# Moving the K and V loads of an attention decode kernel from SyncE's queue to GpSimd, marked as one packet

## The chip, the cores and the metric

The kernel runs on one core of a Trainium2 chip. A core has five engines with instruction streams of their own: TensorE (PE, matmuls and weight loads), VectorE (DVE), ScalarE (ACT), GpSimd (POOL) and SyncE (SP). They meet through semaphores. Data come from HBM, the chip's main memory, into SBUF, the on-chip memory of 128 partitions, by DMA: an engine's instruction stream issues a transfer, and the core's 16 DMA engines carry it out in packets. The metric is the device time of one execution in microseconds (us).

## The reference

One token is decoded. An attention block with 32 heads reads a cache of 65,536 keys and values of 128 elements for each head, a small gated feed-forward block (SwiGLU) reads the same token, and a scalar gate mixes the two.

```python
def _A_ref(x, k_cache, v_cache, wq, wo):
    B, Sq, D = x.shape                      # 1, 1, 512
    H, Dh = 32, 128
    q = (lambda x, *d: x.transpose(*d))((x @ wq).reshape(B, Sq, H, Dh), 0, 2, 1, 3)
    scores = jnp.einsum("bhqd,bhkd->bhqk", q, k_cache) * (Dh ** -0.5)
    p = _softmax(scores, axis=-1)
    o = jnp.einsum("bhqk,bhkd->bhqd", p, v_cache)
    return (lambda x, *d: x.transpose(*d))(o, 0, 2, 1, 3).reshape(B, Sq, H * Dh) @ wo
...
g = _sigmoid((x * gate_w).sum(-1, keepdims=True))
a = _A_ref(x, A_k_cache, A_v_cache, A_wq, A_wo)
b = _B_ref(x, B_w_gate, B_w_up, B_w_down)
return g * a + (1 - g) * b
```

All tensors are bf16. K and V together are about 1.07 GB, and every byte is read once.

## The kernel before, in words

A head's K is 128 partitions by 512 rows of 128 elements. It is cut into two halves, called z = 0 and z = 1, of 256 rows for each partition: 64 KB for each partition, 8.39 MB in all. V is cut the same way. One load brings one half, so a head takes four loads. They all land in one large SBUF tensor, `mem`, which is addressed in units of 1 KB (lines 49, 84 and 109): K's half 0 lies at 32 to 95, its half 1 at 0 to 63 (head 0's half 1 at 96 to 159), V's half 0 at 120 to 183 and its half 1 at 96 to 159. The places overlap, so a load may start only when parts of the half that lies there have been consumed.

**The work of a head.** VectorE transposes a half of K in eight pieces (lines 322, 415 and 422) into the two buffers of `kt`; each transpose adds one to the semaphore `ktdone`. TensorE multiplies each piece with the query (line 472) and adds one to `qkdone`, which allows the transpose after the next. After sixteen pieces the maximum is taken, ScalarE computes the exponentials (line 288), and VectorE spreads them for the value matmuls (line 331). The value matmuls (line 525) come in four parts for each head, and each part adds one to `pvdone`. They run one head behind the scores: in TensorE's loop, head i's scores stand between the parts of head i - 1's values.

**The order of the loads.** SyncE's instruction stream (lines 220 to 263) issues nearly every transfer, so they all go into one queue, q1. The order is written out by hand: first the weights wq, w_gate, w_up, w_down (line 213), then K of head 0 half 0 in two pieces (line 228), then half 1 after the query is ready (`s_q`), then a fixed order in which each load stands behind a wait for the work that frees its place. For head 1's K half 0 that is `ktdone` of 8; for head 0's V half 0, `ktdone` of 13 and `s_b`; for head 1's K half 1, `ktdone` of 20; for head 0's V half 1, `pvdone` of 5. The loop of line 241 repeats the four loads for the next thirty heads (K two heads and V one head ahead of the loop's counter), with waits on constants that grow with the counter. Each load adds 16 to its semaphore when it has landed: `ka`, `kz`, `va`, `vz` for K and V, half 0 and 1.

**The end.** After the loop SyncE waits for `ktdone` of 504 and loads wo (line 251), then the last head's V in eight pieces of falling size (`tail`, line 61, issued on line 258), then two small parts of wo (lines 260 and 261) and the output. GpSimd's stream holds nothing of the kernel's own.

Of the kernel before, what the change touches and what calls it, by code (L numbers as in the profile page):

```python
# [21 lines left out]
def bass_gated_mix__mha_block_cached__swiglu_ffn__decode_kernel(  # L22
# [11 lines left out]
    out: bass.AP,  # L34
):
    _, H, S, Dh = A_k_cache.shape
    D = A_wq.shape[0]
    F = B_w_gate.shape[1]
# [3 lines left out]
    HR = R // 2  # L42
    NP = HR // PR
# [21 lines left out]
    with ExitStack() as ctx:  # L65
# [6 lines left out]
        def sem(name):  # L72
            return ctx.enter_context(nc.semaphore(name))
# [35 lines left out]
        def at(kb, n):  # L109
            return mem[:, kb * KB:kb * KB + n]  # L110
# [7 lines left out]
        mrow, amx, Lt = psM[0:1, 0:128], psM[:, 256:257], psM[:, 257:258]  # L118
        gm = sc[0:1, 5:6]

        names = ("x", "gw", "wq", "wg", "wu", "wd", "ka0", "ka", "kz", "va", "vz", "wo", "wj", "w31")
        d = {n: sem("d_" + n) for n in names}
        dt_ = [sem(f"d_t{i}") for i in range(len(tail))]
        s_ones = sem("s_ones")
# [23 lines left out]
        s_b = sem("s_b")  # L148
        s_dch = sem("s_dch")
        ktdone = sem("ktdone")  # L150
        qkdone = sem("qkdone")
        pvdone = sem("pvdone")
# [48 lines left out]
        def place(kind, h, z):  # L201
            if kind == "k":
                return (KA, V0)[z] if isinstance(h, int) and h == 0 else (KA, KZ)[z]
            return (VA, VZ)[z]

        def kv_dram(cache, h):
            if isinstance(h, int):
                return cache[0, h].rearrange("(b p r) d -> b p (r d)", b=2, p=P)
            return cache[0, ds(h, 1)].rearrange("a (b p r) d -> b (a p) (r d)", b=2, p=P)
# [8 lines left out]
        block = ctx.enter_context(nc.Block())  # L218

        @block.sync  # L220
        def _(sp):
            def load(kind, h, z):
                cache = A_k_cache if kind == "k" else A_v_cache
                sp.dma_start(at(place(kind, h, z), HR * Dh), kv_dram(cache, h)[z]).then_inc(d[kind + "az"[z]], 16)  # L224

            half = HR // 2 * Dh
            for n in range(2):
                sp.dma_start(at(KA + 32 * n, half), kv_dram(A_k_cache, 0)[0][:, n * half:n * half + half]).then_inc(
                    (d["ka0"], d["ka"])[n], 16)
            sp.wait_ge(s_q, 1)  # L230
            load("k", 0, 1)
            sp.wait_ge(ktdone, NP)
            load("k", 1, 0)
            sp.wait_ge(ktdone, 2 * NP - 3)
            sp.wait_ge(s_b, 1)
            load("v", 0, 0)
            sp.wait_ge(ktdone, 2 * NP + NP // 2)
            load("k", 1, 1)
            sp.wait_ge(pvdone, 5)
            load("v", 0, 1)  # L240
            with nc.sync.Fori(0, H - 2) as i:
                sp.wait_ge(ktdone, i * (2 * NP) + (4 * NP - 4))
                load("k", i + 2, 0)
                sp.wait_ge(pvdone, i * 4 + 7)
                load("v", i + 1, 0)
                sp.wait_ge(ktdone, i * (2 * NP) + (4 * NP + NP // 2))
                load("k", i + 2, 1)
                sp.wait_ge(pvdone, i * 4 + 9)
                load("v", i + 1, 1)
            sp.wait_ge(ktdone, 2 * NP * H - NP)  # L250
            sp.dma_start(at(WO, 31 * D), w_dram["wo"][:, 0:31 * D]).then_inc(d["wo"], 16)
            src = A_v_cache[0, H - 1].rearrange("(b p r) d -> b p (r d)", b=2, p=P)
            need = {0: (ktdone, 2 * NP * H - 4), 1: (ktdone, 2 * NP * H), 2: (pvdone, 4 * H - 1)}
            for n, (kb, r0, nr) in enumerate(tail):
                if n in need:
                    sp.wait_ge(*need[n])
                b, o = divmod(r0, HR)
                sp.dma_start(at(kb, nr * Dh), src[b][:, o * Dh:(o + nr) * Dh]).then_inc(dt_[n], 16)
            sp.wait_ge(pvdone, 4 * H)
            sp.dma_start(at(WOJ, D), wj_dram).then_inc(d["wj"], 16)  # L260
            sp.dma_start(at(WO31, D), w31_dram).then_inc(d["w31"], 16)
            sp.wait_ge(s_fin, 1)
            sp.dma_start(out_dram[2:4, :], fin[32:34, :]).then_inc(s_out2, 16)

        @block.scalar
        def _(act):
# [38 lines left out]
        def _(dve):  # L305
# [5 lines left out]
                dve.wait_ge(s_dch, chain[0])  # L311

            def transposes(z):
                dve.wait_ge(d[("ka0", "kz")[z]], 16)
                for c, u in enumerate(k_order[z]):
                    i = NP * z + c
                    if i == NP // 2:
                        dve.wait_ge(d["ka"], 16)
                    if i >= 2:
                        dve.wait_ge(qkdone, i - 1)  # L320
                    src = at(place("k", 0, z) + 8 * u, PR * Dh).bitcast(U32)
                    nc.vector.transpose(kt[:, i % 2, :].rearrange("p (j r t) -> p r j t", j=2, t=32),  # L322
                                        src.rearrange("p (r j t) -> p r j t", j=2, t=32)).then_inc(ktdone, 1)

            def shuffle(z, s):
                c0 = 256 * z
                for g in range(4):
                    for b in range(4):
                        dst = pb[32 * g:32 * g + 32, c0:c0 + 256].rearrange("p (n b) -> p n b", b=4)[:, :, b]
                        sr = pa[32 * b:32 * b + 32, c0:c0 + 256].rearrange("p (n g) -> p n g", g=4)[:, :, g]  # L330
                        last = nc.vector.tensor_copy(dst, sr)  # L331
                last.then_inc(s, 1)

            def top(h, qk):
                dve.wait_ge(qkdone, qk)
                nc.vector.reduce_max(mxs, psS[:], AX_X).then_inc(s_mx, 1)  # L336
                dve.wait_ge(s_mt, h + 1)
                nc.vector.reduce_max(gm, mrow, AX_X).then_inc(s_gm, 1)  # L338

            def late(pv, sl, so):  # L340
                dve.wait_ge(pvdone, pv)
                shuffle(1, s_pbz)
                dve.wait_ge(s_L, sl)
                dve.wait_ge(s_or, so)
                nc.vector.reciprocal(Li, Lt).then_inc(s_li, 1)
# [52 lines left out]
            link(nc.vector.tensor_tensor(hbuf[:, 1, 0:FC], hbuf[:, 0, 0:FC], psM[:, 80:80 + FC], ALU.mult))  # L398
            nc.vector.tensor_scalar(guT[:, 0:FC], hbuf[:, 1, 0:FC], gcol[:, 1:2], None, ALU.mult).then_inc(s_gu, 1)
            transposes(0)  # L400
            transposes(1)
            top(0, 2 * NP)
            with nc.vector.Fori(1, H) as i:
                n = i * (2 * NP)
                v = i * 4
                dma = i * 16
                dve.wait_ge(d["ka"], dma + 16)
                for c, u in enumerate(k_order[0]):
                    if c == NP // 2:
                        dve.wait_ge(expdone, i)  # L410
                        dve.wait_ge(pvdone, v - 2)
                        shuffle(0, s_pba)
                    dve.wait_ge(qkdone, n + (c - 1))
                    src = at(KA + 8 * u, PR * Dh).bitcast(U32)
                    nc.vector.transpose(kt[:, c % 2, :].rearrange("p (j r t) -> p r j t", j=2, t=32),  # L415
                                        src.rearrange("p (r j t) -> p r j t", j=2, t=32)).then_inc(ktdone, 1)
                late(v, i, i)
                dve.wait_ge(d["kz"], dma + 16)
                for c, u in enumerate(k_order[1]):
                    dve.wait_ge(qkdone, n + (NP + c - 1))  # L420
                    src = at(KZ + 8 * u, PR * Dh).bitcast(U32)
                    nc.vector.transpose(kt[:, c % 2, :].rearrange("p (j r t) -> p r j t", j=2, t=32),  # L422
                                        src.rearrange("p (r j t) -> p r j t", j=2, t=32)).then_inc(ktdone, 1)
                top(i, n + 2 * NP)
# [206 lines left out]
```

## Time and profile before

| what | value |
|---|---|
| runs (3), device time | 2513.89 to 2513.92 us, median 2513.9 us |
| profiled execution, span from the first to the last instruction | 2512.4 us |
| median of the runs less the span | 1.5 us |
| granted TensorE clock, mean | 0.721 of full speed |
| HBM read in the profiled execution | 1087.77 MB |

How to read it: the span is one profiled execution; the runs are timed on their own. The page lists busy times of the engines, a strip of 40 equal slices of the span, the DMA queues with their packets, the chain of work that ended last, and the groups of instructions that cost most. The suffix q, as in SPq, marks an engine's instruction stream where it issues a transfer. In a timeline a row is: start, duration, engine, line, operation, output<-input, count, and in brackets the idle time before it with what ended it; repeated instructions are merged, so a row of x2 spans from the first start to the last end.

### The profile page before, as it was taken

Reading aid. Unit: us, or ns where it says so; the run is one execution under the profiler, and the core shown is the slowest. Engines: PE = TensorE matmul, PEld = TensorE weight load, DVE = VectorE, ACT = ScalarE, POOL = GpSimd, SP = SyncE. Lnnn points to the kernel's source line nnn. Section 1 sums busy time; section 2 is a strip of 40 time slices with the busy share of each in tenths; the row PEclk is TensorE's granted clock in tenths of the full one; section 3 lists DMA queues with packets and bytes.
Section 4 is the critical chain, followed back from the end, with each engine's and each line's share of the span. In section 5 each row is a group of like instructions: output and inputs, shape, how many; then the busy total and the mean of one; then the engine's idle time right before and its main releaser. Section 6 shows DMA issues by size and latency. Waiting matters only on the chain.

```text
span 2512.4 us, 51694 instructions
## 1 busy us (share of the span) xinstructions
PE 1709.8 (68%) x21624; PEld 978.8 (39%) x21624; DVE 1411.8 (56%) x1683; ACT 64.6 (3%) x195; POOL 0.2 (0%) x4
## 2 busy tenths in 40 slices
PE   4666766667667677676676766766767767677677
PEld 3334433333433344333443333343334333344334
DVE  4764565554655645646456555465564564645653
ACT  0000000000000000000000000000000000000000
POOL 0000000000000000000000000000000000000000
PEclk8667767777677677776776767767767677677677
DMA  9999999999999999999999999999999999999999
GB/s 420 436 434 434 434 435 434 434 434 434 434 434 434 434 434 434 434 434 434 434 434 434 434 434 434 434 434 434 434 434 434 434 434 434 435 434 434 434 435 402
DMA packets 20470, 1087.93 MB, mean 433 GB/s; under 512 B 2282, under 2 KB 2668, under 8 KB 2924
## 3 DMA queue, kind: packets, MB, share of 16 engines
q1 hardware_dynamic: 20452, 1087.78, 100.0%
q8 instruction: 9, 0.15, 0.0%
q14 instruction: 1, 0.01, 0.0%
q10 hardware_dynamic: 8, 0.00, 0.0%
HBM read 1087.77 MB, written 0.00 MB: 433 GB/s over the span
## 4 chain that ended last, share of the span: by engine, by line
DMA 70%; PE 27%; DVE 1%; issue 1%; SPq 0%; ACT 0%; DVEq 0%
DMA mem<-in_A_v_cache_dram 67%; PE psO L525 27%; DMA mem<-in_A_k_cache_dram 2%; DMA mem<-in_A_wo_dram 1%; DVE kt L322 1%; DMA mem<-in_A_wq_dram 0%; DVE kt L415 0%; SPq L224 0%; PE psM L456 0%; DVE pb L331 0%; PE psS L472 0%; PE psM L547 0%; DVE sm L336 0%; PE psZ L600 0%; PE psM L549 0%
## 5 line engine op out<-in xcount | busy, mean ns | idle before, releaser
L472 PE MATMUL psS<-qcur,kt 128*128 128x4 bf16 x16384 | 573.0, 169 | 728.3 <-DVE kt L415 414.2
L525 PE MATMUL psO<-mem,pb 128*4 128x512 bf16 x3968 | 1040.6, 428 | 32.9 <-DMA mem<-in_A_v_cache_dram 32.6
L472 PEld LDWEIGHTS psS<-qcur,kt 128*128 128x128 bf16 x16384 | 534.0, 105 | 791.9 <-issue 789.5
L422 DVE STREAM_TRANSPOSE kt<-mem 128x2048 uint32<-128x2048 uint32 x248 | 547.6, 2275 | 402.3 <-DMA mem<-in_A_k_cache_dram 402.3
L415 DVE STREAM_TRANSPOSE kt<-mem 128x2048 uint32<-128x2048 uint32 x248 | 551.3, 2280 | 240.3 <-DMA mem<-in_A_k_cache_dram 239.3
L525 PEld LDWEIGHTS psO<-mem,pb 128*4 128x4 bf16 x3968 | 359.4, 93 | 657.5 <-issue 238.4
L331 DVE COPY pb<-pa 32x64 bf16<-32x64 bf16 x1024 | 233.5, 228 | 15.1 <-ACT pa L288 1.5
L338 DVE TENSOR_REDUCE sc<-psM 1x1 f32<-1x128 f32 x32 | 8.9, 279 | 334.9 <-PE psM L547 334.9
L336 DVE TENSOR_REDUCE sm<-psS 128x1 f32<-128x512 f32 x32 | 22.1, 692 | 42.3 <-PE psS L472 42.3
L322 DVE STREAM_TRANSPOSE kt<-mem 128x2048 uint32<-128x2048 uint32 x16 | 35.4, 2277 | 17.0 <-DMA mem<-in_A_k_cache_dram 17.0
L286 ACT ACTIVATE sm<-psM 128x1 f32<-128x1 f32 x32 | 5.5, 171 | 1222.7 <-PE psM L549 1222.7
L282 ACT ACTIVATE oTn<-psT,gcol 128x1 f32 (+1 forms) x31 | 8.2, 264 | 1035.1 <-PE psT L499 1035.1
L499 PE MATMUL psT<-ident,orow 4*128 4x1 f32 x256 | 33.5, 248 | 0.5 <-ACT orow L280 0.5
L499 PEld LDWEIGHTS psT<-ident,orow 4*128 4x128 f32 x256 | 30.8, 186 | 1.2 <-ACT orow L280 0.6
L280 ACT ACTIVATE orow<-psO,sm 4x512 f32<-4x512 f32 x31 | 21.0, 677 | 130.3 <-PE psO L525 126.0
L288 ACT ACTIVATE pa<-psS,sm 128x512 bf16<-128x512 f32 x32 | 22.0, 687 | 1.0
L549 PE MATMUL psM<-sc,onesf 1*128 1x1 f32 x64 | 12.3, 259 | 11.9 <-DVE sc L338 11.9
L561 PE MATMUL psW<-pb,mem 128*128 128x1 bf16 x512 | 14.5, 164 | 5.2 <-DMA mem<-in_A_v_cache_dram 4.7
L549 PEld LDWEIGHTS psM<-sc,onesf 1*128 1x128 f32 x64 | 9.6, 186 | 21.5 <-DVE sc L338 21.5
L561 PEld LDWEIGHTS psW<-pb,mem 128*128 128x128 bf16 x512 | 13.9, 100 | 6.4 <-issue 4.2
L553 PEld LDWEIGHTS psM<-sm,onesf 128*128 128x128 f32 x64 | 9.7, 191 | 14.7 <-issue 13.5
L553 PE MATMUL psM<-sm,onesf 128*128 128x1 f32 x64 | 12.5, 264 | 1.1 <-ACT pa L288 1.1
(72 smaller groups left out, 94.0 us busy)
## 6 DMA issues: line engine op xcount, KB each, us to landing
mem<-in_A_v_cache_dram SPq DMA_DIRECT2D x3, 4096.0 KB, 29.4
mem<-in_A_k_cache_dram SPq DMA_DIRECT2D x2, 4096.0 KB, 38.7
mem<-in_A_wq_dram SPq DMA_DIRECT2D x1, 4096.0 KB, 12.3
mem<-in_A_wo_dram SPq DMA_DIRECT2D x1, 3968.0 KB, 36.7
mem<-in_A_v_cache_dram SPq DMA_DIRECT2D x1, 2048.0 KB, 31.2
mem<-in_B_w_gate_dram SPq DMA_DIRECT2D x1, 1792.0 KB, 16.0
mem<-in_B_w_up_dram SPq DMA_DIRECT2D x1, 1792.0 KB, 21.0
mem<-in_B_w_down_dram SPq DMA_DIRECT2D x1, 1792.0 KB, 24.7
```

The lines of the kernel that those rows point to most:

```text
L288: nc.scalar.activation(pa[:], psS[:], ACT.Exp, bias=nbias, scale=SCALE, accum_out=rsum).then_inc(expdone, 1)
L322: nc.vector.transpose(kt[:, i % 2, :].rearrange("p (j r t) -> p r j t", j=2, t=32), src.rearrange("p (r j t) -> p r j t", j=2, t=32)).then ...
L331: last = nc.vector.tensor_copy(dst, sr)
L336: nc.vector.reduce_max(mxs, psS[:], AX_X).then_inc(s_mx, 1)
L415: nc.vector.transpose(kt[:, c % 2, :].rearrange("p (j r t) -> p r j t", j=2, t=32), src.rearrange("p (r j t) -> p r j t", j=2, t=32)).then ...
L422: nc.vector.transpose(kt[:, c % 2, :].rearrange("p (j r t) -> p r j t", j=2, t=32), src.rearrange("p (r j t) -> p r j t", j=2, t=32)).then ...
L472: last = nc.tensor.matmul(psS[:, o:o + 4] if j is None else psS[:, ds(j * (2 * PR) + o, 4)], ktb[b][:, je // 2, r, :, je % 2], qcur[:, je, ...
L499: last = nc.tensor.matmul(psT[:, 0:1], orow[0:4, i * Dh:(i + 1) * Dh], ident[0:4, i:i + 1], start=(i == 0), stop=(i == 3))
L525: last = nc.tensor.matmul(psO[0:4, :], pb[:, k_col[256 * z + r]:k_col[256 * z + r] + 4], vt[:, r * Dh:(r + 4) * Dh], start=(z == 0 and par ...
L549: nc.tensor.matmul(amx, onesf[0:1, :], gm, start=True, stop=True).then_inc(s_ar, 1)
L553: nc.tensor.matmul(Lt, onesf[:], rsum, start=True, stop=True).then_inc(s_L, 1)
L561: last = nc.tensor.matmul(psW[:, 0:1], vt[:, r * Dh:(r + 1) * Dh], pb[:, col:col + 1], start=(r0 + r == 0), stop=(r0 + r == R - 1))
```

## The change

The loads of K from head 1 on and of V up to head 30, 62 each, leave SyncE's stream and go, with the same waits in the same order, into a stream of GpSimd, with `single_packet=True`. SyncE keeps the weights, all of head 0's K, wo and the pieces of the last head's V. Head 0's K gets semaphores of its own (`ka0`, `ka1`, `kz0`), so that `ka` and `kz` count GpSimd's loads alone, and VectorE's waits for them count from 16 for head 1.

```diff
-        names = ("x", "gw", "wq", "wg", "wu", "wd", "ka0", "ka", "kz", "va", "vz", "wo", "wj", "w31")
+        names = ("x", "gw", "wq", "wg", "wu", "wd", "ka0", "ka1", "kz0", "ka", "kz", "va", "vz", "wo", "wj", "w31")
...
         @block.sync
         def _(sp):
-            def load(kind, h, z):
-                cache = A_k_cache if kind == "k" else A_v_cache
-                sp.dma_start(at(place(kind, h, z), HR * Dh), kv_dram(cache, h)[z]).then_inc(d[kind + "az"[z]], 16)
-
             half = HR // 2 * Dh
             for n in range(2):
                 sp.dma_start(at(KA + 32 * n, half), kv_dram(A_k_cache, 0)[0][:, n * half:n * half + half]).then_inc(
-                    (d["ka0"], d["ka"])[n], 16)
+                    (d["ka0"], d["ka1"])[n], 16)
             sp.wait_ge(s_q, 1)
-            load("k", 0, 1)
-            sp.wait_ge(ktdone, NP)
-            load("k", 1, 0)
...
-            with nc.sync.Fori(0, H - 2) as i:
...
+            sp.dma_start(at(place("k", 0, 1), HR * Dh), kv_dram(A_k_cache, 0)[1]).then_inc(d["kz0"], 16)
             sp.wait_ge(ktdone, 2 * NP * H - NP)
             sp.dma_start(at(WO, 31 * D), w_dram["wo"][:, 0:31 * D]).then_inc(d["wo"], 16)
...
+        @block.gpsimd
+        def _(gp):
+            def gload(kind, h, z):
+                cache = A_k_cache if kind == "k" else A_v_cache
+                gp.dma_start(at(place(kind, h, z), HR * Dh), kv_dram(cache, h)[z],
+                             single_packet=True).then_inc(d[kind + "az"[z]], 16)
+
+            gp.wait_ge(ktdone, NP)
+            gload("k", 1, 0)
+            gp.wait_ge(ktdone, 2 * NP - 3)
+            gp.wait_ge(s_b, 1)
+            gload("v", 0, 0)
+            gp.wait_ge(ktdone, 2 * NP + NP // 2)
+            gload("k", 1, 1)
+            gp.wait_ge(pvdone, 5)
+            gload("v", 0, 1)
+            with nc.gpsimd.Fori(0, H - 2) as i:
+                gp.wait_ge(ktdone, i * (2 * NP) + (4 * NP - 4))
+                gload("k", i + 2, 0)
+                gp.wait_ge(pvdone, i * 4 + 7)
+                gload("v", i + 1, 0)
+                gp.wait_ge(ktdone, i * (2 * NP) + (4 * NP + NP // 2))
+                gload("k", i + 2, 1)
+                gp.wait_ge(pvdone, i * 4 + 9)
+                gload("v", i + 1, 1)
...
             def transposes(z):
-                dve.wait_ge(d[("ka0", "kz")[z]], 16)
+                dve.wait_ge(d[("ka0", "kz0")[z]], 16)
...
-                        dve.wait_ge(d["ka"], 16)
+                        dve.wait_ge(d["ka1"], 16)
...
-                dve.wait_ge(d["ka"], dma + 16)
+                dve.wait_ge(d["ka"], dma)
...
-                dve.wait_ge(d["kz"], dma + 16)
+                dve.wait_ge(d["kz"], dma)
```

More of the change, by code (lines that the diff above doesn't have):

```diff
@@ L228, in _ @@
                 sp.dma_start(at(KA + 32 * n, half), kv_dram(A_k_cache, 0)[0][:, n * half:n * half + half]).then_inc(
-                    (d["ka0"], d["ka"])[n], 16)
+                    (d["ka0"], d["ka1"])[n], 16)
             sp.wait_ge(s_q, 1)
-            load("k", 0, 1)
-            sp.wait_ge(ktdone, NP)
-            load("k", 1, 0)
[L234 to L240, printed above, removed]
-            with nc.sync.Fori(0, H - 2) as i:
[L242 to L249, printed above, removed]
+            sp.dma_start(at(place("k", 0, 1), HR * Dh), kv_dram(A_k_cache, 0)[1]).then_inc(d["kz0"], 16)
             sp.wait_ge(ktdone, 2 * NP * H - NP)
```

## The prediction

> **What bounds the kernel now.** I read the page first: busy times, slices, DMA queues, chain.
>
> ```profile
> span 2512.4 us, 51694 instructions
> PE 1709.8 (68%) x21624; PEld 978.8 (39%) x21624; DVE 1411.8 (56%) x1683; ACT 64.6 (3%) x195; POOL 0.2 (0%) x4
> ...
> DMA  9999999999999999999999999999999999999999
> GB/s 420 436 434 434 434 435 434 434 434 434 434 434 434 434 434 434 434 434 434 434 434 434 434 434 434 434 434 434 434 434 434 434 434 434 435 434 434 434 435 402
> DMA packets 20470, 1087.93 MB, mean 433 GB/s; under 512 B 2282, under 2 KB 2668, under 8 KB 2924
> ...
> q1 hardware_dynamic: 20452, 1087.78, 100.0%
> ...
> DMA 70%; PE 27%; DVE 1%; issue 1%; SPq 0%; ACT 0%; DVEq 0%
> ```
>
> No compute engine is busy above 68%, while the 16 DMA engines are busy in all slices and one queue, q1 (SyncE's), holds 100.0% of their time. The chain that ended last names a load for 70%. The PE share of the chain is no compute bound: the chain passes through the value matmuls because they release the next load, whose bytes then queue behind others. The pace of one load comes from the chain in order of time, whose first steady piece and last one are:
>
> ```profile
> 115.75 27.19 DMA mem<-in_A_v_cache_dram
> ...
> 2433.30 27.91 DMA mem<-in_A_v_cache_dram
> ```
>
> They are the second V loads of heads 0 and 30, so 30 heads take 2317.55 us, 77.25 us a head, **19.31 us** for each of its four loads of 8.39 MB. The line's own view says how early they are issued:
>
> ```profile
> DMA to landing us min/median/max: 26.7/28.4/49.1
> ```
>
> The soonest landing is 26.7 us after its issue, so at least 26.7 - 19.3 = 7.4 us of other loads still stand ahead of it. This lead is why nothing idles. Bytes at a fixed rate bound the kernel: time can only come from a faster stream, and any microsecond in which the DMA engines have no work is lost for good.
>
> **The packets: what can be gained.** The diff moves 124 loads (62 of K, 62 of V) from q1 to GpSimd and marks each as one packet per DMA engine. The DMA view of four narrow windows gives the time of single packets; a share is of 16 engines times the window. In order: 79 to 80 us, 40 to 41 us, 56.5 to 56.7 us, 57.5 to 57.6 us.
>
> ```profile
> q1 hardware_dynamic: 5, 0.33, 75.6%
> ```
> ```profile
> q1 hardware_dynamic: 10, 0.33, 75.8%
> ```
> ```profile
> q8 instruction: 1, 0.02, 29.6%
> ```
> ```profile
> q1 hardware_dynamic: 1, 0.07, 181.2%
> ```
>
> Five 64 KB packets take 0.756 x 16 us / 5 = 2.419 us each, ten 32 KB ones 1.213 us. Two small ones are 2.426, so a packet costs about 7 to 8 ns beside its bytes. Part of that overlaps: 19.31 us / 8 packets is 2.414 us from start to start, some 4 ns less than 2.419. So 4 ns a packet is what joining would save, from 0 to 8 at the ends. A load has 8 packets on each engine (65,536 B x 8 x 16 = 8.39 MB); joining saves 7 boundaries: 7 x 4 ns x 124 = **-3.5 us**, between 0 and -6.9. I take 4, the value nearest to the measured pace.
>
> The Trainium skill (DMA: Bandwidth & Descriptors, "Why small descriptors are slow") gives a fixed overhead of about 3 cycles per packet, which joining descriptors spares. By its figure at 850 MHz the estimate is 3.5 ns, or -3.1 us in place of -3.5; the rows agree.
>
> **A second queue: what a turn costs.** The last two rows above show another queue's transfer among SyncE's loads, the only kind this trace has. A 16 KB instruction fetch took 0.296 x 16 x 0.2 = 0.947 us, where 16 KB at the stream's pace are 0.61; the load's packet after it took 1.812 x 16 x 0.1 = 2.899 us, not 2.419. Out and back cost 0.34 + 0.48 = 0.82 us, about **0.4 us per switch**. It also came in the middle of a load, not behind it: queues take turns between packets.
>
> **The head.** There the order of loads changes. The timelines of SyncE's queue and of VectorE:
>
> ```profile
> 16.72 38.97 SPq L224 DMA_DIRECT2D mem<-in_A_k_cache_dram  x2
> 76.94 0.33 SPq L224 DMA_DIRECT2D mem<-in_A_v_cache_dram  x1
> 95.44 0.33 SPq L224 DMA_DIRECT2D mem<-in_A_k_cache_dram  x1
> ```
> ```profile
> 46.44 8.89 DVE L322 STREAM_TRANSPOSE kt<-mem 128x2048 uint32<-128x2048 uint32 x4 [0.77 <-DMA mem<-in_A_k_cache_dram]
> 65.83 17.66 DVE L322 STREAM_TRANSPOSE kt<-mem 128x2048 uint32<-128x2048 uint32 x8 [10.50 <-DMA mem<-in_A_k_cache_dram]
> ...
> 86.52 8.89 DVE L415 STREAM_TRANSPOSE kt<-mem 128x2048 uint32<-128x2048 uint32 x4
> ```
>
> Call the second half of head 0's K k01 and the first half of head 1's k10. k01 streams from 46.4 and lands at 65.83; k10 is issued at 16.72 + 38.97 - 0.33 = 55.36, when eight transposes are done, waits behind k01, and streams from 65.83 to 85.14. v00, the first V load, is issued at 76.94, 11.11 us after k01 landed (five transposes). It has 8.2 us of lead.
>
> After the change k01 stays on SyncE and k10 comes from GpSimd. GpSimd issues at 55.36 too; its first bytes come L later. The trace has no GpSimd DMA. SyncE's first load is issued at 0.74, and in the DMA view of the first 30 us (slices of 0.75 us) the first bytes are in the third slice, 1.50 to 2.25:
>
> ```profile
> 0.74 0.42 SPq L213 DMA_DIRECT2D mem<-in_A_wq_dram  x1
> ```
> ```profile
> GB/s 0 0 482 218 87 612 612 87 700 262 437 655 87 655 437 262 344 440 440 421 478 363 459 440 404 459 363 459 440 421 440 382 497 751 106 612 655 44 699 306
> ```
>
> That is 0.8 to 1.5 us for SyncE. I take L = 1.5 for GpSimd, and 0.8 to 3.0 (twice the nearest row) for the range. The Trainium skill (same page, "Latency and other measured facts") states 0.6 us for the hardware path and 1 us for GpSimd's; with its 1.0 the sum would be 0.5 us lower.
>
> So k10 is ready at 56.9. k01's fifth packet ends at 46.4 + 5 x 2.41 = 58.5, and three of its eight remain. Now the turn decides. If a marked load is one packet, each engine takes all of k10, 19.31 us, before k01's last three: k01 lands at 65.83 + 19.31 + 0.82 = 85.96. VectorE needs k01 before k10 by program order, so k10's early arrival is of no use. v00's condition is met 11.11 us later at 97.07, its bytes start at 98.57, and the DMA engines have nothing from 85.96 on, since every later load waits behind v00 in GpSimd's order. Before, v00 started at 85.14: **+13.4 us** for everything after it.
>
> What is late next? The fourth load (second half of head 1's K) was issued 95.44 - 65.83 = 29.61 us after k01 landed; now at 115.57, its bytes ready at 117.07, while v00 streams until 117.88. It is in time by 0.8 us, and no second gap opens. Afterwards each issue hangs on a landing, as before, and leads return to 7 us or more: L is hidden there. If GpSimd were slower than that lead, each microsecond beyond it would cost up to 124 us.
>
> The page's section "Queues, rings and completion order" states the rule that the fetch shows only for single packets: an engine drains a whole packet of one ring, then turns to the next. By it the marked load goes whole and the gap is 13.4 us; by the fetch alone it could also alternate 64 KB at a time (second rival).
>
> **The tail.** SyncE no longer stands at the last loads' waits, so wo is issued as soon as ktdone allows:
>
> ```profile
> 2416.06 8.89 DVE L415 STREAM_TRANSPOSE kt<-mem 128x2048 uint32<-128x2048 uint32 x4
> ```
> ```profile
> 2433.30 0.33 SPq L224 DMA_DIRECT2D mem<-in_A_v_cache_dram  x1
> 2433.85 0.34 SPq L251 DMA_DIRECT2D mem<-in_A_wo_dram  x1
> 2450.86 24.83 SPq L258 DMA_DIRECT2D mem<-in_A_v_cache_dram  x8
> ```
>
> That is at 2424.95 instead of 2433.85. One packet of wo may go ahead of the last V load; the pieces of the last head's V follow in the same queue and keep the engines fed, as their issues run until 2475.7, 37 us before the span's end. No gap, three more switches at 0.4: **+1.2 us** (0 if they are hidden). Issue instructions move from SyncE to an idle GpSimd and cost nothing; the renamed semaphores add no wait.
>
> **Sum.** +13.4 + 1.2 - 3.5 = +11.1 on the span of 2512.4, so 2523.5; the runs' median lies 1.5 above the span (2513.9), so **2525.0 us**. With L from 0.8 to 3, switches from none in the tail, and 0 to 8 ns a packet: 2520 to 2530.
>
> **Rivals.**
> (1) *Not slower:* k01 keeps its place, because an engine finishes the descriptors it already holds before it turns to GpSimd's ring. For it: k01's packets were handed over 40 us earlier. Against: the fetch got in mid-load. Decisive point: v00's bytes must be ready by 85.14, so k01 must land by 85.14 - 11.11 - 1.5 = 72.5. Then only the packets count: 2513.9 - 3.5 = 2510.4, from 2507 to 2514. The skill's section "Issuing engines are not separate DMA queues", by which moving issues saves only sequencer time, points to this case.
> (2) *The mark doesn't hold packets together.* Then 64 KB packets alternate: k01's last three need six turns from 58.5 with 6 x 2.41 + 6 x 0.4, and land at 75.4; v00's bytes are ready at 88.0, +2.9. In the tail wo's eight packets alternate too, some 16 switches, 0 to 6.4 us, and nothing is saved: 2516.8 to 2523.2, middle 2520.
> (3) *A bubble at each load:* a marked packet starts only when the one before it is written, as at a switch. 124 x 0.4 = 50 us: 2560. Against it: the page counts 2282 packets under 512 B, some 16 for each load (one per engine, at its end), and the pace holds 434 GB/s across them.
>
> **Chances.** Forecast 0.45 (2520 to 2530), (1) 0.32, (2) 0.14, (3) 0.07, other losses 0.02. A measurement here tells about 0.2%, 5 us, from no change. Faster than 2508.9 needs (1) with more than 5 ns a packet: 0.06. Same: 0.26 of (1) and 0.05 of (2), 0.31. Slower: 0.63. The range 2508 to 2530 takes in all but (3) and the ends.
>
> **What will show it.** In the trace after: VectorE's first transposes of k01 start at 86, not 66; GB/s near zero between about 86 and 98.5; then 434 or 435 without holes; a head in 77.1 us against 77.25, of packets that overlap by more than now or are fewer. I am wrong if k01 lands by 72.5 (rival 1), at about 75 (2), or if the steady rate falls below 434 (3).

## The result, and the profile after

The changed kernel takes **2528.32 us** (median of 4 runs, 2528.09 to 2529.56) against 2513.91 us before (4 runs): 14.4 us more, a ratio of 1.0058 with a 95% interval of 1.0046 to 1.007. The forecast was 2525.0 us, 2520 to 2530 for its own case. The number held; most of the steps to it did not, as the trace shows.

The page of the changed kernel, with the lines that answer to those of before:

```profile
span 2526.8 us, 51725 instructions
...
DMA  9999999999999999999999999999999999999997
GB/s 419 408 431 433 433 433 437 433 438 434 433 432 435 436 436 436 432 433 433 438 433 439 432 433 433 438 432 438 434 433 432 438 433 437 435 433 432 435 434 337
DMA packets 20470, 1087.93 MB, mean 431 GB/s; under 512 B 2282, under 2 KB 2668, under 8 KB 2924
...
q0 software_dynamic: 17856, 1040.20, 95.0%
q1 hardware_dynamic: 2596, 47.58, 4.4%
```

GpSimd's queue is q0. The count of packets is the same to the last one, 20470: the mark has joined nothing that the trace counts. The GB/s strip is low in two places, the second slice (408, before 436) and the last (337, before 402). Between them its slices lie at 431 to 439. GpSimd's timeline gives the time of that steady part; here are three of its first issues and two of the steady part:

```profile
55.93 0.66 POOL L247 DMA_DIRECT2D mem<-in_A_k_cache_dram  x1 [55.36 <-DVE kt L326]
84.67 0.53 POOL L247 DMA_DIRECT2D mem<-in_A_v_cache_dram  x1 [28.07 <-DVE kt L326]
...
123.70 0.53 POOL L247 DMA_DIRECT2D mem<-in_A_v_cache_dram  x1 [20.02 <-PE psO L529]
...
198.46 0.53 POOL L247 DMA_DIRECT2D mem<-in_A_v_cache_dram  x1 [21.01 <-PE psO L529]
...
2438.53 0.53 POOL L247 DMA_DIRECT2D mem<-in_A_v_cache_dram  x1 [20.08 <-PE psO L529]
```

And the row of SyncE's timeline before that stands beside the fourth of them:

```profile
193.23 0.33 SPq L224 DMA_DIRECT2D mem<-in_A_v_cache_dram  x1
```

The second V load of head 1 is issued at 198.46 instead of 193.23, that of head 30 at 2438.53 instead of 2433.30. Both are 5.23 us late: 29 heads take 2240.07 us on either queue. (In the experiments below the same 29 heads take 2240.07 to 2241.77 us, so an issue time places a loss to within some 2 us, not to the hundredth.) So the 14.4 us are **5.2 us of the head, 0.0 of the steady part and 9.2 us of the tail.**

**The head.** VectorE's timeline, and then the DMA view of seven narrow windows (57.3 to 59.7, 60.4 to 62.4, 62.6 to 65.2, 65.2 to 67.6, 67.7 to 70.1, 70.1 to 73 and 85 to 87 us), each row queue, packets, MB and share of the 16 engines:

```profile
73.28 17.66 DVE L326 STREAM_TRANSPOSE kt<-mem 128x2048 uint32<-128x2048 uint32 x8 [17.65 <-DMA mem<-in_A_k_cache_dram]
...
127.34 4.51 DVE L426 STREAM_TRANSPOSE kt<-mem 128x2048 uint32<-128x2048 uint32 x2 [7.80 <-DMA mem<-in_A_k_cache_dram]
```
```profile
q1 hardware_dynamic: 16, 1.05, 103.6%
...
q0 software_dynamic: 15, 0.98, 113.7%
q1 hardware_dynamic: 1, 0.07, 7.6%
...
q1 hardware_dynamic: 15, 0.98, 87.3%
q0 software_dynamic: 1, 0.07, 5.8%
...
q0 software_dynamic: 15, 0.98, 95.9%
q1 hardware_dynamic: 1, 0.07, 6.3%
...
q0 software_dynamic: 13, 0.85, 81.9%
q1 hardware_dynamic: 14, 0.13, 12.9%
...
q0 software_dynamic: 20, 1.31, 104.2%
q1 hardware_dynamic: 4, 0.00, 0.1%
...
q0 software_dynamic: 16, 1.05, 159.0%
```

The queues take turns of one 64 KB packet on each engine: first sixteen packets of q1, then fifteen of q0 and one of q1, then the reverse. A marked load is not one turn. Nor does a turn cost anything: the fifteen q0 packets take 1.137 x 16 x 2 us / 15 = 2.43 us each, as in the steady part. In 67.7 to 70.1 us q1 has its last two 64 KB packets (0.13 MB) and twelve packets of next to no bytes, and in 70.1 to 73 us four more of those. They are the small packets, one per engine, with which a load ends, and they too come only after a turn of q0. Two engines are a packet behind the others, and on them three turns of q0, 3 x 2.42 = 7.3 us, stand ahead of k01's end. So k01 lands at 73.28 us, 7.45 later than before, and v00, which waits for five of its transposes, is issued at 84.67 instead of 76.94. The DMA engines finish k10 between 82.5 and 85 and stand still; when v00 arrives, its first packet on each engine takes 1.59 x 16 x 2 / 16 = 3.18 us (the last row). Two stretches, before and then after (82 to 87 and 120 to 135 us; busy us of PE, PEld, DVE, ACT and POOL, granted clock, DMA share, GB/s):

```profile
82.00:87.00 5.00, 2.83 (x56) 2.17 (x53) 2.95 (x4) 0.00 (x0) 0.00 (x0) 0.50 1.06 459
...
120.00:135.00 15.00, 9.94 (x149) 6.03 (x148) 11.27 (x6) 0.00 (x0) 0.00 (x0) 0.73 0.98 424
```
```profile
82.00:87.00 5.00, 2.64 (x74) 2.49 (x75) 5.00 (x4) 0.00 (x0) 0.53 (x1) 0.50 0.76 262
...
120.00:135.00 15.00, 14.80 (x176) 7.89 (x174) 5.56 (x3) 0.00 (x0) 0.53 (x1) 0.89 0.97 393
```

A second weak stretch follows at 120 to 135 us, 393 GB/s for 424 before. There the next V load is issued at 123.70, with less than half of its old lead: the second K half of head 1, which streams ahead of it, lands at 127.34, 3.6 us later, where before it was 8.0 (115.75 and 123.73).

**The tail.** The chain of work that ended last, in order of time, and SyncE's timeline:

```profile
2438.53 41.88 DMA mem<-in_A_v_cache_dram
...
2480.45 11.18 PE psO L529 x40
...
2517.46 6.92 PE psW L565 x256
```
```profile
2429.96 0.33 SPq L229 DMA_DIRECT2D mem<-in_A_wo_dram  x1
2462.93 31.62 SPq L236 DMA_DIRECT2D mem<-in_A_v_cache_dram  x8
```

The last V load of head 30 lands 41.88 us after its issue, not 27.91. wo and the first pieces of the last V took turns with it and with the K load before it. The DMA view of 2436 to 2442 us shows the turns of wo (q1):

```profile
q0 software_dynamic: 25, 1.64, 63.0%
q1 hardware_dynamic: 24, 0.76, 29.4%
```

About as many packets of one queue as of the other, but 64 KB each on q0 and 0.76 MB / 24 = 32 KB on q1: a turn is one packet, of 64 KB or of half as much. From the landing at 2480.41 TensorE works without waiting for a load, 46.4 us to the end of the span. A small part of these goes with the clock: the 31 matmuls of psY take 9.60 us here, at a granted clock of 0.69 (2503 to 2513 us), and took 8.17 before, at 0.81 (2484 to 2493 us). Before, the end hung on the last bytes; the last load in the chain of work was this one:

```profile
2479.22 30.75 DMA mem<-in_A_wo_dram
```

Now it hangs on the landing of one V load, and the DMA engines are idle at the end (337 GB/s in the last slice).

### The profile page after: what moved, and what is told of

The parts are those of the page before. It is cut to its first block, busy times and chain, and to the rows that moved or that the text cites. A ratio compares the mean times of both kernels' runs of the same rounds, so it can differ in the third digit from the quotient of the medians.

```text
span 2526.8 us, 51725 instructions
## 1 busy us (share of the span) xinstructions
PE 1707.2 (68%) x21624; PEld 977.8 (39%) x21624; DVE 1412.2 (56%) x1683; ACT 64.7 (3%) x195; POOL 67.1 (3%) x128
## 2 busy tenths in 40 slices
DMA packets 20470, 1087.93 MB, mean 431 GB/s; under 512 B 2282, under 2 KB 2668, under 8 KB 2924
## 4 chain that ended last, share of the span: by engine, by line
DMA 66%; PE 28%; DVE 2%; issue 2%; another core or an unknown queue 1%; POOLq 0%; SPq 0%; ACT 0%; DVEq 0%
DMA mem<-in_A_v_cache_dram 65%; PE psO L529 27%; DMA mem<-in_A_k_cache_dram 2%; DVE kt L326 1%; PE psW L565 0%; DVE kt L419 0%; PE psY L580 0%; DVE kt L426 0%; DVE pb L335 0%; PE psS L476 0%; POOLq L247 0%; SPq L213 0%; PE psT L503 0%; PE psZ L588 0%
## 5 line engine op out<-in xcount | busy, mean ns | idle before, releaser
L247 POOL DMA_DIRECT2D mem<-in_A_v_cache_dram x62 | 32.9, 530 | 1293.5 <-PE psO L529 1241.5
L247 POOL DMA_DIRECT2D mem<-in_A_k_cache_dram x62 | 34.0, 548 | 1078.1 <-DVE kt L419 519.3
```

Source lines behind the costliest of these rows:

```text
L247: gp.dma_start(at(place(kind, h, z), HR * Dh), kv_dram(cache, h)[z], single_packet=True).then_inc(d[kind + "az"[z]], 16)
```

## The experiments

Theory A: two queues alternate packet by packet (64 KB for K and V), mark or no mark; in the head and the tail this delays the load that the next work needs. Theory B: the mark does something. Theory C: GpSimd as the issuer costs the time. Times are medians; the kernel before, run beside them, lay at 2513.79 to 2513.88.

**1. The mark.**

```diff
-                gp.dma_start(at(place(kind, h, z), HR * Dh), kv_dram(cache, h)[z],
-                             single_packet=True).then_inc(d[kind + "az"[z]], 16)
+                gp.dma_start(at(place(kind, h, z), HR * Dh), kv_dram(cache, h)[z]).then_inc(d[kind + "az"[z]], 16)
```

> The changed kernel without the one-packet mark; all else as it is. Theory A (two queues alternate 64 KB at a time at the head and at the tail, mark or no mark, and this order costs the time): 2528.3 us as with the mark, within 1 us, loads in the steady part 19.32 us apart, and the first half 1 of K lands at 73 us. Theory B (the mark does something: it saves some ns at each packet or it changes the turns): the pace differs by 0.03 us a load, 3.5 us in all (2531.8 us), or K of head 0 half 1 lands at another time by several us.

Measured: 2528.34 us, against 2528.32 with the mark. VectorE's timeline and GpSimd's last issue:

```profile
73.18 17.67 DVE L325 STREAM_TRANSPOSE kt<-mem 128x2048 uint32<-128x2048 uint32 x8 [17.72 <-DMA mem<-in_A_k_cache_dram]
```
```profile
198.10 0.53 POOL L247 DMA_DIRECT2D mem<-in_A_v_cache_dram  x1 [21.37 <-PE psO L528]
...
2438.37 0.53 POOL L247 DMA_DIRECT2D mem<-in_A_v_cache_dram  x1 [20.21 <-PE psO L528]
```

The landing is the same within 0.1 us, and 29 heads take 2240.27 us. The DMA view of 60.4 to 62.5 and 62.6 to 65.2 us shows the turns themselves:

```profile
q0 software_dynamic: 16, 1.05, 115.1%
...
q1 hardware_dynamic: 16, 1.05, 93.0%
```

B falls: on these loads the mark changes neither pace nor turns.

**2. The head in one queue.** GpSimd issues head 0's K half 1 too.

```diff
-            sp.wait_ge(s_q, 1)
-            sp.dma_start(at(place("k", 0, 1), HR * Dh), kv_dram(A_k_cache, 0)[1]).then_inc(d["kz0"], 16)
...
+            gp.wait_ge(ktdone, 3)
+            gp.dma_start(at(place("k", 0, 1), HR * Dh), kv_dram(A_k_cache, 0)[1],
+                         single_packet=True).then_inc(d["kz0"], 16)
             gp.wait_ge(ktdone, NP)
```

> Only the head is put back in one order: GpSimd issues head 0's K half 1 too, at three transposes, ahead of head 1's K. Theory A: K half 1 of head 0 lands at 66 to 67 us and not 73, V of head 0 is issued at about 78 us, the hole of 3 us before it goes, and so does the slow stretch at 125 to 133 us, which only followed from the late start: 4.7 us less, 2523.6 us (2522.5 to 2525). Theory C (GpSimd as the issuer costs the time, wherever the loads begin): 2527 to 2528 us.

Measured: 2526.27 us, 2.05 less than the changed kernel and not 4.7. VectorE's timeline, and GpSimd's:

```profile
69.11 17.66 DVE L327 STREAM_TRANSPOSE kt<-mem 128x2048 uint32<-128x2048 uint32 x8 [13.41 <-DMA mem<-in_A_k_cache_dram]
```
```profile
80.49 0.53 POOL L245 DMA_DIRECT2D mem<-in_A_v_cache_dram  x1 [23.95 <-DVE kt L327]
```

v00 is now issued at 80.49, while k10, which follows K half 1 at the pace of 19.3 us, streams until about 69.1 + 19.3 = 88.4: the hole before v00 has gone. But K half 1 lands at 69.11, not at 66 to 67, still 3.3 us later than before: handing the stream from one queue to the other left a hole of its own (experiments 4 and 5 show it). So the direction speaks for A, the size was missed.

**3. The tail in one queue.** wo and the pieces follow the last load in GpSimd's stream (the same lines with `gp` for `sp`, behind the loop).

```diff
-            sp.wait_ge(ktdone, 2 * NP * H - NP)
-            sp.dma_start(at(WO, 31 * D), w_dram["wo"][:, 0:31 * D]).then_inc(d["wo"], 16)
...
+            gp.wait_ge(ktdone, 2 * NP * H - NP)
+            gp.dma_start(at(WO, 31 * D), w_dram["wo"][:, 0:31 * D]).then_inc(d["wo"], 16)
```

> Only the tail is put back in one order: wo and the pieces of the last V are issued by GpSimd behind its last load. Theory A: the last load of V of head 30 lands about 20 us after the K load before it, instead of 28, and the end is bound by the bytes again: 9 us less, 2519.3 us (2518.5 to 2520.5). Theory C: 2527 to 2528 us.

Measured: 2519.39 us (2517.41 to 2521.5, 10 runs), 8.9 less. The chain in order of time, from a run of 2517.55 us, one of the shortest of the ten:

```profile
2437.41 27.50 DMA mem<-in_A_v_cache_dram
...
2478.93 34.23 DMA mem<-in_A_v_cache_dram
```

The last V load of head 30 takes 27.50 us again, and the end hangs on bytes again (its second row).

**4 and 5. Both in one queue**, with the first GpSimd load at three transposes, and at two. The two differ in one line:

```diff
-            gp.wait_ge(ktdone, 3)
+            gp.wait_ge(ktdone, 2)
```

> Head and tail both in one order on GpSimd. Theory A: nothing is left of the loss but the head's small changes: 2514.5 us (2513.5 to 2516), no faster than before, since the pace of a load is 19.32 us on either queue. Theory B with a saving at each packet: 2510.5 us. Theory C: 2526 us or more.

> Head and tail both on GpSimd, with its first load issued at two transposes instead of three, 2.2 us earlier. In the version with three the DMA engines stood still for 0.5 us at the handover and the first packets took 3.2 us instead of 2.42. Theory A: with the first load ready before SyncE's last one has ended both go: 2515.5 us (2514.5 to 2516.3), still not under the kernel before. If the first packets of a new queue are slow in any case: 2516.5 to 2517.

Measured: 2516.8 us with three, 0.8 above the expected range; 2515.72 us with two (ratio to before 1.0007, interval 0.9998 to 1.0017). The DMA view of 44 to 47 us of the first of them, in slices of 0.075 us:

```profile
GB/s 0 0 0 0 0 0 0 0 437 0 0 0 0 437 0 0 0 0 1748 4369 2621 874 0 874 1748 0 0 0 0 0 874 0 0 0 0 0 0 874 0 0
...
q0 software_dynamic: 16, 1.05, 105.4%
```

Bytes are counted where a packet starts: most engines start their first q0 packet together, at 45.4 us, and the sixteen take 1.054 x 16 x 3 / 16 = 3.16 us each instead of 2.42. That is the handover which the expectation of experiment 2 left out. With the load ready earlier 1.1 us come back, and not all of it: issued at 42.11, the load takes turns with the K load before it, whose second piece lands at 49.58 instead of 46.68 us. Both kernels issue all steady loads from GpSimd, and they are within about 0.1% of the kernel before: C falls. No version tried was faster than before.

**6. The tail's second queue without GpSimd's steady loads.** The kernel before; only wo and the pieces go to GpSimd.

```diff
+        @block.gpsimd
+        def _(gp):
+            gp.wait_ge(ktdone, 2 * NP * H - NP)
+            gp.dma_start(at(WO, 31 * D), w_dram["wo"][:, 0:31 * D]).then_inc(d["wo"], 16)
...
```

> The kernel before, with all steady loads on SyncE as they were; only wo and the pieces of the last V are issued by GpSimd, at the same conditions. Theory A (two queues alternate, whichever holds the steady loads): the head is as before; the last K load lands some 25 us after the one before it and the last V load of head 30 some 26.5 us after that, 13 us late together, and from that landing TensorE's work needs 46.4 us to the end, as in the changed kernel: 2522 us (2521 to 2524). Theory C (GpSimd's steady loads cost the time): 2514 to 2515 us.

Measured: 2522.22 us, 8.4 above before. The chain:

```profile
2433.21 42.39 DMA mem<-in_A_v_cache_dram
```

It is issued at 2433.21, as before, and lands at 2475.60; from there to the end of the span at 2521.9 are 46.3 us. The roles of the queues are reversed, and the loss is nearly the same (9.2 us in the changed kernel).

**7 and 8. Less of the second stream beside the last loads.** In the changed kernel SyncE waits for V of head 30: in experiment 7 ahead of wo, as shown, and in experiment 8 with the same line behind wo, ahead of the pieces.

```diff
             sp.wait_ge(ktdone, 2 * NP * H - NP)
+            sp.wait_ge(d["vz"], 16 * (H - 1))
             sp.dma_start(at(WO, 31 * D), w_dram["wo"][:, 0:31 * D]).then_inc(d["wo"], 16)
```

> The changed kernel; SyncE waits until V of head 30 has landed before it issues wo, so no bytes of the tail go beside the last two loads. Theory A: these two land 19.32 us apart again, then the DMA engines start anew with a gap of about 2 us, and the end is bound by bytes: 2521 us (2520 to 2523), 2 us above the version with the tail on GpSimd. If the tail's loss came from something else than the alternation (late issues, PE's own work), 2528 us or more.

> The changed kernel; wo is issued as there, but the pieces of the last V wait until V of head 30 has landed: a smaller dose of the same. Theory A: the last K load still lands 25 us after the one before (wo beside it), V of head 30 only about 23 us after that instead of 26.5, and the end comes 3.6 us earlier, as TensorE's 46.4 us from that landing set it: 2524.7 us (2523.5 to 2526). Without the alternation as the cause: 2528 us.

Measured: 2522.52 us with no bytes beside, 2524.93 us with wo alone, 2528.32 us with all of it. The last V load of head 30 in the three chains took 27.44, 37.05 and 41.88 us; the rows of the first two:

```profile
2438.45 27.44 DMA mem<-in_A_v_cache_dram
```
```profile
2438.40 37.05 DMA mem<-in_A_v_cache_dram
```

The time goes with the dose, and no transfer has changed its issuer. In experiment 8 two errors of the expectation offset each other: the load landed at 2475.45, 5.0 us sooner than in the changed kernel where 3.6 were expected, but from there to the end of the span at 2523.9 were 48.4 us, not 46.4; why the end took longer is not shown. With experiments 3 and 6 the cause of the tail's loss is shown: bytes of a second queue beside the last loads.

**9. The head's second queue without GpSimd.** The kernel before; head 1's K half 0 is issued by ScalarE.

```diff
-            sp.wait_ge(ktdone, NP)
-            load("k", 1, 0)
...
+            act.wait_ge(ktdone, NP)
+            act.dma_start(at(place("k", 1, 0), HR * Dh), kv_dram(A_k_cache, 1)[0]).then_inc(d["ka"], 16)
             exps(0)
```

> The kernel before with one load moved and no GpSimd at all: head 1's K half 0 is issued by ScalarE, in its own queue, at the same condition, while head 0's K half 1 streams in SyncE's. Theory A (any second queue alternates with the first, 64 KB at a time): head 0's K half 1 lands at 73 us, V of head 0 is issued at 84 us instead of 77, the DMA engines stand still for about 1.7 us around 84 to 85.5 and their first packets are 0.7 us slower: 2516.3 us (2515.5 to 2518). Theory C (GpSimd's queue is what alternates or costs): 66 us for that landing and 2513.9 us.

Measured: 2519.72 us (11 runs, 2517.51 to 2520.36), 5.8 above before. VectorE's timeline, and SyncE's:

```profile
73.21 17.66 DVE L322 STREAM_TRANSPOSE kt<-mem 128x2048 uint32<-128x2048 uint32 x8 [17.64 <-DMA mem<-in_A_k_cache_dram]
```
```profile
84.32 0.33 SPq L224 DMA_DIRECT2D mem<-in_A_v_cache_dram  x1
...
124.21 0.33 SPq L224 DMA_DIRECT2D mem<-in_A_v_cache_dram  x1
...
2439.49 0.33 SPq L224 DMA_DIRECT2D mem<-in_A_v_cache_dram  x1
```

The landing at 73.21 and the issue at 84.32 are as A has them, with a hardware queue in GpSimd's place. The price is not: 5.8 us, where 2.4 were expected. The last load of the loop is issued 2439.49 - 2433.30 = 6.19 us late, so all of it arises at the head. The expectation had left out the second weak stretch, at 120 to 135 us. That stretch goes with the issue of the V load there: issued at 123.20 (experiment 3) the stretch has 437 GB/s, at 123.61 (experiment 7) 415, at 123.70 (the changed kernel) 393, at 124.21 (this one) 376. Whether those few tenths decide it was not tried by itself.

## Why the number held and the reasons did not

**What bounds the kernel** held. The pace of a load is the same in every version to within 0.1% (29 heads in 2240.07 to 2241.77 us), and the holes at the head stayed in the time.

**The packets, -3.5 us:** mis-sized; the term is 0.0. The bounds from 0 to -6.9 held, the value taken did not. The rows gave rightly that a packet costs some ns beside its bytes; the step that failed is that the mark takes this away. 29 heads take 2240.07 us with it on GpSimd, 2240.07 without it on SyncE, 2240.27 without it on GpSimd.

**A second queue, 0.4 us a switch:** wrong. What was read off an instruction fetch does not carry over to loads: packets of both queues in turns take 2.43 us.

**The head, +13.4 us:** the mechanism was right up to the size of a turn, and that was the step that failed: "each engine takes all of k10, 19.31 us, before k01's last three". A turn is 64 KB, so k01 landed at 73.28 and not at 85.96. The second rival had this, with 75.4; without its price of a switch its six turns end at 58.5 + 6 x 2.41 = 73.0. Its count of three turns came out right for the two engines that are a packet behind the others and set the landing (on the other fourteen, k01's first packet starts before 45 us in both kernels, not at 46.4), although two of its steps did not hold: no packet of q0 started before 60.4 us, 4.5 us after the issue at 55.93 and one packet later than counted, and the third turn stood ahead of the small end packets.

The Trainium skill (DMA: Bandwidth & Descriptors, "Queues, rings and completion order") states that an engine drains a whole packet of one ring, typically 9 to 17 descriptors, before it switches. The trace shows the switch after every single 64 KB packet, with the mark and without.

GpSimd's delay L held where nothing stood in its way: v00's first packets start at 85.9, 1.5 us after its condition was met (73.28 + 11.11 = 84.39), the value taken, and 1.2 us after the start of its issue at 84.67. The Trainium skill's figure of 1 us ("Latency and other measured facts") is close to the 1.2.

**What is late next:** "no second gap opens" failed. For the fourth load it was right. The fifth waits for the first part of the values. The prediction let each later issue hang on a landing; in the trace the late K half decided: v00 landed 23.2 us after its issue, at 107.9, and these matmuls began at 112.83, 7.46 us later than before (105.37), just as k01 was. So the load came at 123.70 with 3.6 us of lead, and of the 5.2 us some 1.6 were lost there (the fourth load landed at 127.34 instead of 123.73, 3.6 late; the steady part runs 5.2 late).

**The tail, +1.2 us:** an eighth of the 9.2 us measured. "The pieces of the last head's V follow in the same queue and keep the engines fed" was true until they ran out: what follows in a second queue also goes beside the first queue's last load. That load landed 14 us later relative to its issue, and the pieces from the third on wait for the values that it feeds. The prediction counted the bytes, which were all there, and did not ask which of them the end was waiting for.

**The rivals.** The first (k01 keeps its place) fell with the landing at 73.28. The second had the right turns, at the head nearly the right size (+2.9), but let the tail cost only switches. The third fell with the steady pace. So the sum met the result by luck: a head 8.2 us too dear, a tail 8.0 us too cheap and a saving of 3.5 us that did not come left 3.3 us between them.

## What to carry to other kernels

Moving some transfers to another queue removes an order that the program relied on: bytes of both queues share the engines from the moment the second is issued. Before moving them, look at each place where both queues hold work, and ask which of the two transfers the next work waits for; where it is the older one, keep both in one queue. A sum of bytes tells when the stream ends, but the end of the kernel may hang on one landing in the middle of it.

## What the runs showed of the hardware that was not expected

- The one-packet mark on loads whose 64 KB rows each are one packet changed neither the count of packets (20470), the turns nor the pace (2240.07 and 2240.27 us).
- The small packets that end a load wait for a turn like the others: k01's last 64 KB packets started by 70.1 us, and four of its end packets only after that, behind packets of q0.
- Packets that start on all engines at once after a hole take 3.1 to 3.2 us instead of 2.42, on GpSimd's queue (159.0% in 85 to 87 us) and with SyncE's as well. In experiment 9, 85.2 to 87 us, 1.716 x 16 x 1.8 / 16 = 3.09 us:

```profile
q1 hardware_dynamic: 16, 1.05, 171.6%
```

- The changed versions spread more from run to run: the kernel before spreads over 0.6 us in 15 runs beside experiment 9, that experiment over 2.9 us in 11, experiment 3 over 4.1 in 10. The cause is not shown; the short lead of the V load at 120 to 135 us is not all of it, since experiment 4, where that load is issued 7.1 us before the landing ahead of it (118.78 and 125.88), still spreads over 2.4 us in 10.
